# Retention and feed-forward on one core: two retention clusters per group against one, with a GpSimd token between its two output parts

## The chip, the cores and the metric

The kernel runs on one core of a Trainium2 chip. A core has five engines that work side by side, each through its own queue of instructions in order: TensorE (PE in the profile, its weight loads PEld), VectorE (DVE), ScalarE (ACT), GpSimd (POOL) and SyncE (SP), which here issues almost all transfers. They meet only through semaphores: an instruction may wait for counts that other engines or transfers raise. Tiles live in SBUF, on 128 partitions; TensorE writes its results into PSUM, which has eight banks of 512 float32 per partition.

The metric is the device time of one execution in microseconds, the median of several runs. For the kernel before it is 292.66 us (five runs, 292.35 to 292.84). One execution was also taken with the hardware profiler.

## What is computed

A retention layer (attention with a decay in place of a softmax) and, on its output, a feed-forward layer with a squared relu:

```python
# q, k, v: (8, 8, 576, 64)   w_in: (512, 2048)   w_out: (2048, 512)
scores = scale * np.matmul(q, k.transpose(0, 1, 3, 2))
gamma = 1.0 - 2.0 ** (-5.0 - np.arange(H, dtype=np.float32))
Dmat = np.where(rel >= 0, gamma[:, None, None] ** rel[None, :, :], 0.0)
ret = scores * Dmat[None, :, :, :]
attn = np.matmul(ret, v)
x = attn.transpose(0, 2, 1, 3).reshape(B * S, H * D)
r = np.maximum(x @ w_in, 0.0)
out = (r * r) @ w_out
```

Inputs and output are float32; the kernel's matmuls work in fp16.

## The kernel before

**Units and groups.** The 576 positions of a batch are cut into four full units of 128 positions and a rest of 64; the rests of two batches make one tail unit. That gives 36 units, taken two at a time in 18 groups (0 to 17). Units 8, 17, 26 and 35 are tails. Units below 8 (groups 0 to 3) are handled in pairs by other functions, which the change doesn't touch.

**Retention of a unit.** The decay is split into factors of the position, so that a unit needs only a 64x64 masked product inside each half (a chunk) and a running state between chunks. Per unit: GpSimd casts k, q and v to fp16 (`add_unit`; L366 k and q, L378 v with its decay); SyncE transposes k and q by a DMA (L391) into `kqT`. TensorE then makes, in 64x64 pieces through `quad` (L354): *scores* (`psc`, 16 matmuls a unit, bank pair prS), *sums* of k times v for the state (`psS`, 16 for a full unit, none for a tail), and the output `psO` (bank pair prO) in two parts, *out1* and *out2*. out1 and half of out2 multiply q with the states `R` and `Rm`; the other part of out2 multiplies v with the masked scores `rT`. out1 and out2 add into the same places of PSUM from different halves of the array's rows. VectorE masks the scores (`rT`, L658), builds the states (`Rm` L677 and L679, `stmp` L683, `R` L687) and scales the output into `xT` (L719).

`quad` gives TensorE a position in the array: a 64x64 quarter. Everything else on TensorE (feed-forward, transposes of the paired units) uses the whole 128x128 array. A run of 64x64 matmuls between such work is called a cluster here.

**Clusters before.** `add_ret` builds them. For groups 4 to 6 there are two a group: scores and sums of the group, and later out1, a drain of TensorE, and out2. From group 7 (`JOIN = 7`) on the work of neighbouring groups is joined in another way: a first cluster has out1 of group g and scores of g+1, a second, some 2 to 5 us later, has sums of g+1 (into the bank pair prS, after the scores there have been masked) and out2 of g. Group 17 has its outputs alone, with a drain.

**Feed-forward of a group.** `add_ff`: 64 matmuls of 256 columns with w_in (L842, into `ph`, one PSUM bank for eight of them), relu on ScalarE (L850), square on ScalarE for seven of eight banks (L860) or on VectorE (L862), and from group 2 on the second matmul by Strassen's scheme (`add_strassen`): seven products of eight matmuls (L934) on fp16 sums `gS` that VectorE builds (L911), with copies on ScalarE (L947, L1008) and adds on VectorE (L957) into `o`, which SyncE stores. `ph`, the products' `po` and the transposes share the four feed-forward banks (tag "ff").

**What sets the order.** Every piece of work is a task of the class `Schedule`, with an engine, a key (priority), an assumed duration, tasks that it depends on and resources that it takes (`acq`: ff 4, prS 1, prO 1, and counts of buffers). `emit` plays the tasks through with the assumed durations and writes them out in the order in which they started. On the chip each engine works through its list in that order, and semaphores hold it where something is not ready. So a changed key, resource or duration can move instructions on every engine.

Of the kernel before, what the change touches and what calls it, by code (L numbers as in the profile page):

```python
# [15 lines left out]
class Schedule:  # L16
# [4 lines left out]
        self.count = dict(count)  # L21
        self.tasks = []

    def add(self, eng, key, dur, fn, deps=(), acq=(), after=None, lag=0.0):
        t = dict(eng=eng, key=key, dur=dur, fn=fn, acq=acq, n=len(self.tasks), users=[], free=[], lag=lag,
                 left=len(deps), ready=0.0, lat=self.LAT[eng] if after is None else after)
        for d in deps:
            d["users"].append(t)
        self.tasks.append(t)
        return t  # L30
# [11 lines left out]
    def emit(self):  # L42
        ready = {e: [] for e in self.LAT}
        busy = {e: False for e in self.LAT}
        events = []
        order = []
        seq = 0

        def push(at, what, t):
            nonlocal seq  # L50
            seq += 1
            heapq.heappush(events, (at, seq, what, t))
        for t in self.tasks:
            if t["left"] == 0:
                heapq.heappush(ready[t["eng"]], (t["key"], t["n"], t))
        now = 0.0
        while True:
            for e in ready:
                if busy[e]:
                    continue  # L60
                held = []
                while ready[e]:
                    item = heapq.heappop(ready[e])
                    t = item[2]
                    if all(self.count[r] >= t["acq"].count(r) for r in t["acq"]):
                        for r in t["acq"]:
                            self.count[r] -= 1
                        t["start"] = now
                        order.append(t)
                        busy[e] = True  # L70
                        push(now + t["dur"], "end", t)
                        break
                    held.append(item)
                for item in held:
                    heapq.heappush(ready[e], item)
            if not events:
                break
            now = events[0][0]
            while events and events[0][0] <= now + 1e-9:
                _, _, what, t = heapq.heappop(events)  # L80
                if what == "end":
                    busy[t["eng"]] = False
                    for w in t["users"]:

                        push(now + (0.0 if w["eng"] == t["eng"] else t["lat"]), "dep", w)
                    for g in t["free"]:
                        push(now + t["lat"], "free", g)
                elif what == "dep":
                    t["left"] -= 1
                    if t["left"] == 0:  # L90
                        push(now + t["lag"], "go", t)
                elif what == "go":
                    heapq.heappush(ready[t["eng"]], (t["key"], t["n"], t))
                else:
                    t["left"] -= 1
                    if t["left"] == 0:
                        self.count[t["res"]] += 1
        assert len(order) == len(self.tasks)
        for t in order:
            t["fn"]()  # L100
# [3 lines left out]
def kernel(  # L104
# [9 lines left out]
    nc = tc.nc  # L114
# [44 lines left out]
    w_out16 = const.tile([P, NF, DM], FP16, name="w_out16")  # L159


    junk = const.tile([P, 512], FP16, name="junk")
    nc.vector.memset(junk, 0.0)
    ident = const.tile([P, P], FP16, name="ident")
    make_identity(nc, ident)
# [28 lines left out]


    heads = [(4 * n + 2 * a + b, n, a, b) for n in range(2) for a in range(2) for b in range(2)]
    lncol = const.tile([P, NP], FP32, name="lncol")
    lnrow_R = const.tile([P, NP], FP32, name="lnrow_R")
    for h, n, a, b in heads:
        nc.vector.memset(lncol[64 * b:64 * b + 64, 2 * n + a:2 * n + a + 1], lng[h])  # L200
        nc.vector.memset(lnrow_R[64 * a:64 * a + 64, 2 * n + b:2 * n + b + 1], lng[h])

    mask = const.tile([P, 64], FP32, name="mask")
    nc.gpsimd.memset(mask, 1.0)
    for c in range(2):
        nc.gpsimd.affine_select(out=mask[c * 64:(c + 1) * 64], in_=mask[c * 64:(c + 1) * 64],
                                compare_op=ALU.is_ge, fill=0.0, base=0, pattern=[[1, 64]], channel_multiplier=-1)

    mask2 = const.tile([P, 2, 2, 64], FP32, name="mask2")
    nc.gpsimd.memset(mask2, 1.0)  # L210
    for c in range(2):
        for e in range(2):
# [4 lines left out]
    for hp in range(NP):  # L217
# [9 lines left out]
    SQ_ACT = (0, 1, 2, 3, 4, 5, 6)  # L227
    SPREAD = 0.1
    SQ_LATE = (1, 4, 6)
    JOIN = 7  # L230
    LAG = {"v2": 1.2, "w1": 1.3, "k4": 0.7, "q4": 0.5}
    LAG_T, LAG_O = 1.5, 5.0
    PAIRED = 8
    FIRST = ["k0", "q0", "v0", "k2", "q2", "w0", "v2", "w1", "w2", "w3", "w4", "w5", "w6", "w7", "k4", "q4", "v4", "k6", "q6", "v6"]
    sched = Schedule(dict(ff=4, prS=1, prO=1, g=3, ld=5, wst=4, kq=7, v16=7, rT=4, x=3, rl=3, o=4, p1=2, u2=2, u4=2,
                          R=6, Rm=6, kqT=6))
    add = sched.add
    tile_of = {}
    last_load = []
# [110 lines left out]

    def quad(out_, lhsT, rhs, row, col, start=True):
        nc.tensor.matmul(out_, lhsT=lhsT, rhs=rhs, start=start, stop=True, skip_group_check=True,  # L354
                         tile_position=(64 * row, 64 * col))

    def half(x):
        return slice(64 * x, 64 * x + 64)
# [1 line left out]
    def add_unit(u, base):  # L360
# [15 lines left out]
        def fv():  # L376
# [1 line left out]
            nc.gpsimd.tensor_tensor(  # L378
                out=t, in0=tile_of["v32", u],
                in1=vdec[kind].rearrange("p (h o) -> p h o", o=1).to_broadcast([P, H, D]), op=ALU.mult)  # L380
        ck = add("POOL", base, 0.65, fk, deps=[loaded["k", u]], acq=("kq",))
        cq = add("POOL", base + 1, 0.62, fq, deps=[loaded["q", u], ck])
        cv = add("POOL", base + 2, 1.1, fv, deps=[loaded["v", u]] + tail, acq=("v16",))
        for what, t in (("k", ck), ("v", cv)):
            for w in gate.get((what, u), []):
                sched.need(w, t)
# [201 lines left out]
    def emit_sums(g, tag):  # L588

        if not full_of(g):  # L590
            return
        tile_of["psS", g] = ps_ret.tile([P, 2, 512], FP32, name="psS", tag=tag)
        for s, u in enumerate(units_of(g)):
            if u not in full_of(g):
                continue
            ps = tile_of["psS", g][:, :, cols(s)].rearrange("p c (n i) -> p c n i", i=64)
            for hp in range(NP):
                for c, a in ((0, 0), (1, 1), (0, 1), (1, 0)):
                    h = 4 * (hp // 2) + 2 * a + hp % 2
                    quad(ps[half(a), c, hp, :], tile_of["kq", u][half(c), 0, half(2 * hp + a)],  # L600
                         tile_of["v16", u][half(c), h, :], c, a)


# [61 lines left out]
    def after_sums(g, t, key, res):  # L665

        chain = []
        for s, u in enumerate(units_of(g)):
            if u not in full_of(g):
                continue  # L670
            c0 = units[u][2] == 0

            def fr0(s=s, u=u, c0=c0):
                r = tile_of["Rm", u] = st_pool.tile([P, NP * D], FP16, name="Rm", tag="Rm")
                x = tile_of["psS", g][:, 0, cols(s)]
                if c0:
                    nc.vector.tensor_copy(out=r, in_=x)  # L677
                else:
                    nc.vector.tensor_tensor(out=r, in0=x, in1=tile_of["R", u - 1], op=ALU.add)  # L679

            def fr1(s=s, u=u):
                r = tile_of["tmp", u] = work.tile([P, NP * D], FP32, name="stmp", tag="stmp", bufs=1)
                nc.vector.tensor_tensor(out=r, in0=tile_of["psS", g][:, 1, cols(s)], in1=tile_of["Rm", u], op=ALU.add)  # L683

            def fr2(s=s, u=u):
                r = tile_of["R", u] = st_pool.tile([P, NP * D], FP16, name="R", tag="R")
                nc.vector.tensor_tensor(  # L687
                    out=r.rearrange("p (n d) -> p n d", d=D), in0=tile_of["tmp", u].rearrange("p (n d) -> p n d", d=D),
                    in1=dec128.rearrange("p (n o) -> p n o", o=1).to_broadcast([P, NP, D]), op=ALU.mult)
            r0 = add("DVE", key + 0.1 + s, 0.42, fr0, deps=[t] + chain[-1:] + ([] if c0 else [T["R", u - 1]]),  # L690
                     acq=("Rm",))
            if not c0:
                T["Rread", u - 1].append(r0)
            r1 = add("DVE", key + 0.2 + s, 0.42, fr1, deps=[r0])
            r2 = add("DVE", key + 0.3 + s, 0.5, fr2, deps=[r1], acq=("R",))
            chain += [r0, r1, r2]
            T["Rm", u], T["R", u], T["Rread", u], T["Rmread", u] = r0, r2, [], r1
        if chain:
            sched.free(res, [chain[-2]])

    def after_outs(g, t1, t2, key):
# [33 lines left out]
    def add_ret(g):  # L735
# [15 lines left out]
            after_scores(g, t, base + 5)  # L751
            after_sums(g, t, base + 5, "prO")
        if joined(g):
            k = len(groups[g + 1])

            def f1():
                emit_out1(g)
                emit_scores(g + 1)

            def f2():  # L760

                emit_sums(g + 1, "prS")
                emit_out2(g)
            t1 = add("PE", base + 10, 0.2 + QUAD * (8 * n + 16 * k), f1, deps=out1_deps(g) + scores_deps(g + 1),
                     acq=("prO", "prS"))
            after_scores(g + 1, t1, base + 11)
            t2 = add("PE", base + 30, 0.2 + QUAD * (24 * n + 16 * len(full_of(g + 1))), f2,
                     deps=[t1] + T["masked", g] + T["masked", g + 1] + sums_deps(g + 1), acq=("prS",))
            for u in units_of(g + 1):
                T["kqread", u] = t2  # L770
            after_outs(g, t1, t2, base + 30.4)
            after_sums(g + 1, t2, base + 31, "prS")
        else:
            def fb():
                emit_out1(g)
# [7 lines left out]

    HF, HM = NF // 2, DM // 2
    wB = {(i, j): w_out16[:, i * HF:(i + 1) * HF, j * HM:(j + 1) * HM] for i in range(2) for j in range(2)}
    wT = [const.tile([P, HF, HM], FP16, name=f"wT{i}") for i in range(4)]

    def add_wT(i, in0, in1):
        ts = []
# [284 lines left out]
```

## Time and profile before

| What | Value |
|---|---|
| median of five runs | 292.66 us |
| the profiled execution, its own time | 292.8 us |
| its span, first to last instruction | 291.08 us |
| TensorE clock granted | 1.00 |
| wide matmuls with w_in (L842, 128x256) | 1152 |
| wide matmuls of the second layer (L934, 128x256) | 896 |
| relu on ScalarE (L850) | 144 x 589 ns |
| square on ScalarE (L860) | 104 x 631 ns |
| copy of a bank's half on ScalarE (L947, 128x256) | 48, 365 to 370 ns |
| cast of k or q on GpSimd (L366) | 28 + 28, 672 ns mean |
| cast of v on GpSimd (L378, full units) | 24 x 1067 ns |
| xT on VectorE (L719) | 28 x 685 ns |
| mask of scores on VectorE (L658) | 28 x 682 ns |
| transposing DMA (L391), issue to landing | 3.1 / 4.3 / 6.0 us (min, median, max) |

The page lists busy time by engine and by line. For TensorE a matmul's "busy" time is longer than its share of the pace, since matmuls overlap; the distance from one start to the next is the pace. In the timeline each row has the start in us, the length in us, engine, line, operation, output, inputs, shape, count and, in brackets, how long the engine was idle before and what ended that.

### The profile page before, as it was taken

How to read it: one execution, taken by the hardware profiler on the slowest of the kernel's cores; microseconds unless marked ns; L12 is line 12 of the kernel's file. 1: busy time of each engine (PE TensorE's matmuls, PEld its weight loads, DVE VectorE, ACT ScalarE, POOL GpSimd, SP SyncE). 2: the span in 40 equal slices, each digit the busy share in tenths (PEclk: the TensorE clock that was granted, in tenths of full speed). 3: DMA queues.
4: the chain of work that ended last, by engine and by line, in shares of the span. 5: the costliest groups of instructions: out<-in, count | busy, mean ns of one | idle time of the engine just before them, and what ended most of it. 6: DMA issues, size and time to landing. Idle time of an engine off the chain costs nothing.

```text
span 291.1 us, 10071 instructions
## 1 busy us (share of the span) xinstructions
PE 283.5 (97%) x4328; PEld 233.8 (80%) x4328; DVE 197.5 (68%) x430; ACT 187.5 (64%) x356; POOL 89.2 (31%) x125
## 2 busy tenths in 40 slices
PE   7999999999999999999999999999999999999995
PEld 3557765588888888888888888888888888888884
DVE  3877379849495958766768856666786866564632
ACT  6366876385757575867666666756767676747830
POOL 4352455515414333441604241505061500000000
PEclk9999999999999999999999999999999999999999
DMA  7999999999999999998959899959897920201004
GB/s 194 326 351 387 375 283 257 218 189 187 243 159 224 202 178 245 212 219 202 183 141 206 185 215 211 196 146 192 189 184 197 166 77 2 74 2 73 2 0 146
DMA packets 139949, 54.14 MB, mean 186 GB/s; under 512 B 118144, under 2 KB 131968, under 8 KB 139904
## 3 DMA queue, kind: packets, MB, share of 16 engines
q1 hardware_dynamic: 139600, 53.23, 81.1%
q8 instruction: 34, 0.56, 0.8%
q10 hardware_dynamic: 304, 0.26, 0.3%
q14 instruction: 11, 0.09, 0.1%
HBM read 36.70 MB, written 9.44 MB: 159 GB/s over the span
## 4 chain that ended last, share of the span: by engine, by line
PE 89%; DMA 6%; SPq 2%; DVE 1%; issue 1%; POOL 0%; DVEq 0%
PE ph L842 43%; PE po L934 34%; DMA wi<-in_moe_w_in_dram 6%; PE po L882 4%; PE psO L354 4%; SPq L298 2%; PE psc L354 2%; PE psS L354 2%; DVE rx L472 1%; POOL w_in L333 0%; PE psT L429 0%; DVE o L957 0%; DVE p L986 0%; DVE stmp L495 0%; DVE R L500 0%
## 5 line engine op out<-in xcount | busy, mean ns | idle before, releaser
L842 PE MATMUL ph<-xT,w_in 128*128 128x256 f16 x1152 | 139.9, 273 | 0.4 <-POOL w_in L333 0.4
L842 PEld LDWEIGHTS <-w_in 128*128 128x128 f16 x1152 | 110.9, 98 | 15.9 <-POOL w_in L333 0.9
L850 ACT ACTIVATE rl<-ph 128x512 f16<-128x512 f32 x144 | 84.1, 589 | 47.2 <-PE ph L842 45.4
L860 ACT ACTIVATE gT<-rl 128x512 f16<-128x512 f16 x104 | 65.6, 631 | 2.9
L934 PEld LDWEIGHTS <-gS 128*128 128x128 f16 x512 | 49.2, 98 | 6.7 <-DVE gS L911 0.8
L934 PE MATMUL po<-wT,gS 128*128 128x256 f16 x384 | 52.5, 273 | 0.0
L911 DVE TENSOR_TENSOR gS<-gT,gS 128x512 f16<-128x512 f16 x64 | 34.8, 549 | 11.2 <-ACT gT L860 10.6
L934 PEld LDWEIGHTS <-gT 128*128 128x128 f16 x384 | 37.2, 98 | 4.4
L911 DVE TENSOR_TENSOR gS<-gT 128x512 f16<-128x512 f16 x64 | 32.3, 505 | 12.5 <-ACT gT L860 12.4
L934 PE MATMUL po<-w_out,gT 128*128 128x256 f16 x256 | 34.5, 273 | 0.0
L366 POOL CAST kq<-k 128x512 f16<-128x512 f32 x28 | 18.8, 672 | 47.0 <-DMA k<-in_k_dram 40.3
L366 POOL CAST kq<-q 128x512 f16<-128x512 f32 x28 | 18.8, 673 | 44.6 <-DMA q<-in_q_dram 44.5
L862 DVE TENSOR_TENSOR gT<-rl 128x512 f16<-128x512 f16 x40 | 20.6, 519 | 15.7 <-ACT rl L850 15.0
L378 POOL TENSOR_TENSOR v<-v,vdec_full 128x512 f16<-128x512 f32 x24 | 25.6, 1067 | 18.1 <-DMA v<-in_v_dram 16.5
L947 ACT COPY u<-po 128x256 f32<-128x256 f32 x32 | 11.8, 370 | 21.5 <-PE po L934 21.4
L957 DVE TENSOR_TENSOR o<-po,u 128x256 f32<-128x256 f32 x31 | 13.0, 421 | 15.5 <-PE po L934 7.8
L719 DVE TENSOR_TENSOR xT<-psO,gam_full 128x512 f16<-128x512 f32 x28 | 18.9, 685 | 6.0 <-PE psO L354 6.0
L658 DVE TENSOR_TENSOR rT<-psc,mask 128x512 f16<-128x512 f32 x28 | 18.3, 682 | 5.7 <-PE psc L354 5.7
L934 PE MATMUL po<-wT,gT 128*128 128x256 f16 x128 | 17.0, 273 | 0.0
L934 PE MATMUL po<-w_out,gS 128*128 128x256 f16 x128 | 16.9, 273 | 0.0
L882 PE MATMUL po<-w_out,gT 128*128 128x512 f16 x64 | 16.0, 380 | 0.3 <-DVE stmp L495 0.3
L957 DVE TENSOR_TENSOR o<-po,p 128x256 f32<-128x256 f32 x17 | 7.2, 424 | 12.0 <-ACT u L947 5.2
(81 smaller groups left out, 244.5 us busy)
## 6 DMA issues: line engine op xcount, KB each, us to landing
out_dram<-o SPq DMA_DIRECT2D x31, 256.0 KB, 3.4
k<-in_k_dram SPq DMA_DIRECT2D x24, 256.0 KB, 4.4
q<-in_q_dram SPq DMA_DIRECT2D x24, 256.0 KB, 4.8
v<-in_v_dram SPq DMA_DIRECT2D x24, 256.0 KB, 5.0
wo<-in_moe_w_out_dram SPq DMA_DIRECT2D x4, 1024.0 KB, 9.7
wi<-in_moe_w_in_dram SPq DMA_DIRECT2D x3, 1024.0 KB, 8.9
pair<-in_k_dram SPq DMA_DIRECT2D x4, 512.0 KB, 6.9
pair<-in_q_dram SPq DMA_DIRECT2D x4, 512.0 KB, 7.3
```

The source lines that it names most:

```text
L354: nc.tensor.matmul(out_, lhsT=lhsT, rhs=rhs, start=start, stop=True, skip_group_check=True, tile_position=(64 * row, 64 * col))
L366: op(out=out_.rearrange("p (n b a d) -> p n b a d", n=2, b=2, a=2), in_=in_.rearrange("p (n a b) d -> p n b a d", n=2, a=2))
L378: nc.gpsimd.tensor_tensor(out=t, in0=tile_of["v32", u], in1=vdec[kind].rearrange("p (h o) -> p h o", o=1).to_broadcast([P, H, D]), op=ALU. ...
L719: nc.vector.tensor_tensor(out=tile_of["x", g][:, :, s * P:(s + 1) * P].rearrange("p n (c i) -> p c n i", c=2), in0=tile_of["psO", g][:, :, ...
L842: nc.tensor.matmul(tile_of["ph", g, fb][:, j, :], lhsT=w_in16[:, m, fi * P:(fi + 1) * P], rhs=tile_of["x", g][:, m, :], start=(m == 0), st ...
L850: nc.scalar.activation(out=t, in_=tile_of["ph", g, fb], func=ACTF.Relu)
L860: nc.scalar.activation(out=t, in_=rl, func=ACTF.Square)
L862: nc.vector.tensor_tensor(out=t, in0=rl, in1=rl, op=ALU.mult)
L882: nc.tensor.matmul(tile_of["po", u], lhsT=tile_of["g", g][:, fi, s * P:(s + 1) * P], rhs=w_out16[:, fi, :], start=(fi == 0), stop=(fi == N ...
L911: nc.vector.tensor_tensor(out=Sx(k, h), in0=in0(h), in1=in1(h), op=op)
L934: nc.tensor.matmul(tile_of["pb", g, bank], lhsT=left(i), rhs=right[:, i, :], start=(start and i == 0), stop=(i == HF - 1), skip_group_chec ...
L957: nc.vector.tensor_tensor(out=o_tile(u)[:, half * HM:(half + 1) * HM], in0=bank(x), in1=tile_of[name, g], op=ALU.add)
```

## The change

- `JOIN` is 5: groups 5 to 16 are joined.
- A joined group has one cluster instead of two: out1 of g, scores of g+1, sums of g+1, out2 of g, in this order.
- Between out1 and out2 a GpSimd instruction (`pass_turn`: a memset of one element, `token`) waits for out1's last matmul, and out2's first matmul waits for it.
- The sums go into two feed-forward banks (one per row half) in place of prS. If both units of g+1 are full, ScalarE copies the second unit's half of both banks into an SBUF tile `sums`, from which VectorE builds that unit's state.
- The planner gets a resource "pool" (1), which the casts of units from 8 on and the joined cluster take in turn, and a flag `firm`: a firm task that waits for resources keeps others from taking them.
- Keys change: the cluster's (`CLUSTER = 26`), those of masks, `xT` and the second part of the states (`K_MASK`, `K_X`, `K_ST`).
- `junk`, the operand of the warm-up matmuls, is now part of `wT[0]`, and the masks are fp16.

In the order that results, TensorE has the same stream up to group 4's output, and the same matmuls after that. On GpSimd there are 12 memsets, each behind the casts that its cluster reads (five of them behind one or two casts of the next unit too); on SyncE some transposes, stores and loads change places.

```diff
-    def add(self, eng, key, dur, fn, deps=(), acq=(), after=None, lag=0.0):
+    def add(self, eng, key, dur, fn, deps=(), acq=(), after=None, lag=0.0, firm=False):
...
+        kept = {}
+        LASTING = ("pool",)
...
+                kept = {r: t for r, t in kept.items() if r in LASTING}
...
-                    if all(self.count[r] >= t["acq"].count(r) for r in t["acq"]):
+                    if all(kept.get(r, t) is t for r in t["acq"]) and all(self.count[r] >= t["acq"].count(r) for r in t["acq"]):
...
+                            kept.pop(r, None)
...
+                    if t["firm"]:
+                        kept.update((r, t) for r in t["acq"] if r not in kept)
...
-    junk = const.tile([P, 512], FP16, name="junk")
+    wT = [const.tile([P, NF // 2, DM // 2], FP16, name=f"wT{i}") for i in range(4)]
+    junk = wT[0][:, 0:2].rearrange("p f m -> p (f m)")
...
-    mask = const.tile([P, 64], FP32, name="mask")
+    mask = const.tile([P, 64], FP16, name="mask")
...
-    JOIN = 7
+    JOIN = 5
+    CLUSTER = 26
+    K_MASK, K_X, K_ST = 30, 8, 30
...
+    def pass_turn():
+        last = issued[-1]
+        mark = nc.gpsimd.memset(token, 0.0)
+        after(mark, last)
+        return mark
...
-        ck = add("POOL", base, 0.65, fk, deps=[loaded["k", u]], acq=("kq",))
-        cq = add("POOL", base + 1, 0.62, fq, deps=[loaded["q", u], ck])
-        cv = add("POOL", base + 2, 1.1, fv, deps=[loaded["v", u]] + tail, acq=("v16",))
+        ck = add("POOL", base, 0.65, fk, deps=[loaded["k", u]], acq=("kq", "pool"))
+        cq = add("POOL", base + 1, 0.62, fq, deps=[loaded["q", u], ck], acq=("pool",))
+        cv = add("POOL", base + 2, 1.1, fv, deps=[loaded["v", u]] + tail, acq=("v16", "pool"))
+        for x in (ck, cq, cv):
+            sched.free("pool", [x])
...
-        tile_of["psS", g] = ps_ret.tile([P, 2, 512], FP32, name="psS", tag=tag)
+        if tag == "ff":
+            tile_of["psS", g] = [ps_ff.tile([P, 512], FP32, name="psS", tag="ff") for c in range(2)]
...
+        aside = res == "ff" and len(us) == 2
+        copies = {}
+        if aside:
+            def fc(c):
+                def f():
+                    if c == 1:
+                        tile_of["sums", g] = work.tile([P, 2, 256], FP32, name="sums", tag="sums", bufs=1)
+                    nc.scalar.copy(out=tile_of["sums", g][:, c], in_=tile_of["psS", g][c][:, cols(1)])
+                return f
+            copies[1] = add("ACT", key, 0.37, fc(1), deps=[t], acq=("sums",))
+            copies[0] = add("ACT", key + 0.01, 0.37, fc(0), deps=[copies[1]])
...
+        if aside:
+            sched.need(copies[0], chain[0])
+            sched.free("ff", [copies[0]])
+            sched.free("ff", [chain[1]])
+            sched.free("sums", [chain[-2]])
...
         if joined(g):
-            k = len(groups[g + 1])
-
-            def f1():
+            n1 = len(full_of(g + 1))
+
+            def f():
                 emit_out1(g)
+                mark = pass_turn()
                 emit_scores(g + 1)
-
-            def f2():
-
-                emit_sums(g + 1, "prS")
+                emit_sums(g + 1, "ff")
+                turn.append(mark)
                 emit_out2(g)
-            t1 = add("PE", base + 10, 0.2 + QUAD * (8 * n + 16 * k), f1, deps=out1_deps(g) + scores_deps(g + 1),
-                     acq=("prO", "prS"))
-            after_scores(g + 1, t1, base + 11)
-            t2 = add("PE", base + 30, 0.2 + QUAD * (24 * n + 16 * len(full_of(g + 1))), f2,
-                     deps=[t1] + T["masked", g] + T["masked", g + 1] + sums_deps(g + 1), acq=("prS",))
+            t = add("PE", base + CLUSTER, 0.17 + QUAD * (32 * n + 16 * len(groups[g + 1]) + 16 * n1), f,
+                    deps=out1_deps(g) + T["masked", g] + scores_deps(g + 1) + sums_deps(g + 1),
+                    acq=("prO", "prS", "pool") + (("ff", "ff") if n1 else ()), firm=True)
+            sched.free("pool", [t])
+            after_scores(g + 1, t, base + CLUSTER + K_MASK)
             for u in units_of(g + 1):
-                T["kqread", u] = t2
-            after_outs(g, t1, t2, base + 30.4)
-            after_sums(g + 1, t2, base + 31, "prS")
+                T["kqread", u] = t
+            after_sums(g + 1, t, base + CLUSTER + 0.5, "ff")
+            after_outs(g, t, t, base + CLUSTER + K_X)
```

## The prediction, made before the changed kernel ran

> **What bounds the kernel now.** I read the page first (busy shares, slices, the chain that ended last), then the timeline of TensorE around the lines that the diff touches, then the rows that price a signal between engines.
>
> ```profile
> PE 283.5 (97%) x4328; PEld 233.8 (80%) x4328; DVE 197.5 (68%) x430; ACT 187.5 (64%) x356; POOL 89.2 (31%) x125
> ...
> PE   7999999999999999999999999999999999999995
> ...
> PEclk9999999999999999999999999999999999999999
> ...
> PE 89%; DMA 6%; SPq 2%; DVE 1%; issue 1%; POOL 0%; DVEq 0%
> ```
>
> From about 25 us to the end TensorE never rests, at full clock, and the chain is 89% TensorE. So an edit counts for what it does to TensorE's own stream, or if it makes TensorE wait. The timeline shows where the stream has holes:
>
> ```profile
> 152.14 1.04 PE L934 MATMUL po<-w_out,gT 128*128 128x256 f16 x8
> 153.02 1.04 PE L934 MATMUL po<-wT,gS 128*128 128x256 f16 x8
> 153.89 1.47 PE L842 MATMUL ph<-xT,w_in 128*128 128x256 f16 x12
> ...
> 158.69 1.04 PE L934 MATMUL po<-wT,gS 128*128 128x256 f16 x8
> 159.66 0.21 PE L354 MATMUL psO<-kqT,Rm 64*64 64x64 f16 x1
> ...
> 160.17 0.61 PE L842 MATMUL ph<-xT,w_in 128*128 128x256 f16 x4
> 160.62 1.04 PE L934 MATMUL po<-w_out,gS 128*128 128x256 f16 x8
> 161.49 1.04 PE L934 MATMUL po<-wT,gT 128*128 128x256 f16 x8
> 162.46 0.45 PE L354 MATMUL psS<-v,kq 64*64 64x64 f16 x32
> ...
> 163.23 3.67 PE L842 MATMUL ph<-xT,w_in 128*128 128x256 f16 x32
> ```
>
> The first column is the start, so starts give the pace. Sixteen wide matmuls take 1.75 us (152.14 to 153.89): 0.109 each, 0.875 for eight. Where 64x64 work follows, eight take 0.97 (158.69 to 159.66; 161.49 to 162.46): entering a retention cluster costs 0.095. Inside, the 48 small matmuls of the group's first cluster take 0.51 and the 80 of its second 0.77 (to 163.23). The difference gives 0.0081 for a small matmul, and 0.51 - 48 x 0.0081 = 0.12 is fixed. A cluster thus costs 0.21 us beside its matmuls. I find no other hole of weight: outside clusters the wide matmuls keep 0.109, with three slips of 0.1 to 0.2 us after 64 us.
>
> **The change, part by part.**
>
> 1. *Fewer clusters.* Before, groups 7 to 16 have two each. After, one with the same small matmuls (16 out1, 32 scores, 32 sums, 48 out2; fewer with tail units): 10 x 0.21 = 2.1 us saved.
>
> 2. *Groups 5 and 6 join.* Before, outputs 5, scores and sums 6, outputs 6, scores and sums 7 are four clusters. After, two: 2 x 0.21 = 0.42. Also gone are the two drains between the output parts:
>
> ```profile
> 87.10 0.19 PE L354 MATMUL psO<-kqT,Rm 64*64 64x64 f16 x1
> ...
> 87.39 0.32 PE L354 MATMUL psO<-rT,v 64*64 64x64 f16 x16
> ...
> 87.99 0.61 POOL L366 CAST kq<-k 128x512 f16<-128x512 f32 x1 [1.15 <-PE psO L354]
> 88.11 1.29 DVE L719 TENSOR_TENSOR xT<-psO,gam_full 128x512 f16<-128x512 f32 x2 [0.32 <-PE psO L354]
> ```
>
> Group 5's cluster takes 0.93 for 64 matmuls (86.97 to 87.90), where 64 without a drain take 0.65 (94.55 to 95.20): 0.28. Group 6's takes 0.90 for 56 (102.05 to 102.95) against 0.12 + 56 x 0.0081 = 0.57: 0.33. Together 0.61. Parts 1 and 2: 2.1 + 0.42 + 0.61 = 3.13 us off.
>
> 3. *The token.* In each of the 12 joined clusters GpSimd waits for out1's last matmul, writes one element, and the first weight load of out2 waits for that. Four steps, from rows: a small matmul takes 0.19 (87.10). TensorE's end to GpSimd's start: the last small matmul ends at 87.97, the cast starts at 87.99: 0.02. From the second token on the instruction carries two waits; VectorE's xT, with two, starts 0.14 after 87.97, so I add 0.1. The write itself and GpSimd to TensorE:
>
> ```profile
> 0.31 0.10 POOL L1058 MEMSET const-float32-0.0<- 128x1 f32 x1 [0.31 <-issue]
> ...
> 18.38 1.57 POOL L410 TENSOR_TENSOR vx<-pair,vdec_pair 128x512 f16<-128x512 f32 x1 [2.13 <-DMA pair<-in_v_dram]
> ...
> 20.00 0.29 PE L354 MATMUL psS<-vx,kx 64*64 64x64 f16 x12 [0.61 <-POOL vx L410]
> ```
>
> 0.10, and 0.05 (19.95 to 20.00). Sum 0.19 + 0.02 + 0.10 + 0.10 + 0.05 = 0.46 from the start of out1's last matmul. The cover is scores and sums: 65 steps x 0.0081 = 0.53 in nine clusters, 49 x 0.0081 = 0.40 in the three whose next group has a tail unit (7, 12, 16). An exposed weight load adds something (its row is 0.11, of which 0.02 to 0.05 shows, by the spacing of the first rows of a cluster). I take 0.03 x 9 + 0.10 x 3 = 0.57. Bounds: 0 (all covered) and 0.1 x 9 + 0.18 x 3 = 1.44 (the whole weight load exposed).
>
> What stands ahead of the token in GpSimd's queue are the casts of the group that the cluster needs anyway, and in some clusters from group 10 on one or two casts of the next unit. Behind it wait the next six casts, 2 x (0.67 + 0.67 + 1.07) = 4.8 us of GpSimd, and behind them on SyncE two transposes (4.3 us to landing, up to 6.0) and the stores and loads queued after them. Next late would be the next cluster's scores. For units 16 and 17: cluster 6 at about 104.4 (TensorE's order at the pace above), token over by 105, fifth cast 3.8 later, transpose landed by 115, cluster 7 at about 117.3. So 2 us remain where this is tightest, and I take 0. If that cover were gone, TensorE would wait the excess in each cluster.
>
> 4. *A GpSimd write against VectorE.* [...]
>
> ```profile
> 77.65 1.04 POOL L378 TENSOR_TENSOR v<-v,vdec_full 128x512 f16<-128x512 f32 x1 [0.42 <-DMA v<-in_v_dram]
> 78.13 0.85 DVE L911 TENSOR_TENSOR gS<-gT,gS 128x512 f16<-128x512 f16 x1 [1.87 <-ACT gT L860]
> 78.64 0.81 POOL L366 CAST kq<-k 128x512 f16<-128x512 f32 x1
> ```
>
> The add takes 0.85 instead of 0.42, the cast 0.81 instead of 0.61. A token behind one add would be up to 0.42 late. But in VectorE's new order only PSUM-reading adds (o<-po) stand between the last such add and the cluster, group 5 apart. Bounds 0 and 12 x 0.42 = 5.0; nearest is the PSUM-reading add (0.41 beside casts, nobody stretched), so 0 here, kept as a rival. [...]
>
> 5. *Sums in feed-forward banks.* They hold two of four. ScalarE copies out the second unit's half: 2 x 0.37 a cluster, nine full clusters, 6.7 us on an engine 64% busy; hidden, since its long waits are for ph (45.4 us). If that cover were gone, 0.74 a cluster. VectorE runs add (0.42), x (0.69), add (0.42), x (0.69): both banks are back some 1.7 us after the cluster, x is done at 2.3. TensorE fills a ph bank per 0.875, so it wants the third at 1.75; x is wanted earliest in group 5, after 12 ph and 16 po matmuls, 3.06. Banks are the close call: bounds 0 and 0.25 x 12 = 3.0 (one slip like the largest seen); by the three slips now, 0.2 in all. VectorE's two adds from the SBUF copy may stretch from 0.42 to 0.85 beside casts: 0.86 a cluster at 68% busy, hidden; uncovered, they would make the Strassen sums late.
>
> 6. *Small edits.* A weight load with two waits takes 0.05 on TensorE's queue; five clusters now have one in mid-stream, 0 to 0.25, I take 0.13. The fp16 masks (0.68 now; nearest all-fp16 add 0.42), junk inside wT touch no wait of TensorE. Scores come some 3 us later in a group, and masks (after x) and states behind them; all are read only in the next cluster, some 14 us on: 0; uncovered, each us late would be a us of that cluster's wait.
>
> Sum: -3.13 + 0.57 + 0.2 + 0.13 = -2.23 us. The profiled span 291.08 becomes 288.85. That execution took 292.8, the median of the runs is 292.66; what lies around the span stays, so 292.66 - 2.23 = **290.4**. Extremes without the rivals: 292.66 - 3.13 = 289.5, and with 1.44, 0.25 and 0.6 of bank slips, 291.8.
>
> **The rivals.**
>
> *A: the fixed 0.12 is paid per part, not per cluster.* Each cluster now has two parts, the new one four. Against it: the 64-matmul cluster (0.65) and the 80-matmul one fit one line. For it: none has four parts. Then only 0.095 a cluster goes: 12 x 0.095 + 0.61 = 1.75; with costs of 0.9, 292.66 - 0.85 = 291.8.
>
> *B: the banks eat it.* Two banks out of four gone for 1.7 us while ScalarE (7 of 8 squares) works off relu. A slip of 0.25 in every cluster gives back 3.0, so 292.66 - 2.23 - 0.2 + 3.0 = 293.2 at worst; with half, 291.7. It decides from 0.19 a cluster (2.23 / 12): no change, 292.6. For it: x, sums and copies crowd just there. Against: no ph wait of weight in 144 banks now.
>
> *C, the slower side: the token is late.* If a cast or an fp16 add holds GpSimd when out1 ends, TensorE stands in mid-cluster. At 0.42 in each of twelve: 292.66 - 2.23 + 5.0 = 295.4. It turns slower once the token is 0.19 later than I count. For it: GpSimd works in order, and its casts wait for DMA 107 us in sum. Against: its casts for a cluster now end 8 to 14 us before the scores.
>
> **How the numbers follow.** Forecast 0.65 (own range 289.5 to 291.4), A 0.12, B 0.11, C 0.12. A measurement of this kernel tells 0.2% (0.59 us) from no change. Faster takes the forecast, three quarters of A and a little of B: 0.76; the rest of A and most of B: 0.12 same; C: 0.12 slower. The range runs from 289.4, all hidden, to 292.4, which takes in A and half of B and leaves C out.
>
> **What would show it.** Right: one cluster per group from the sixth, 128 small matmuls in about 1.2 us with a step below 0.1 before out2; 12 clusters fewer; no drain within groups 5 and 6; wide matmuls still at 0.109 after a cluster; span near 288.9. Wrong: a hole of 0.2 or more before out2 with GpSimd as releaser (C); ph weight loads that wait for ScalarE or VectorE after a cluster (B); more than 1.4 us without one hole (A); scores that wait for kqT.

## The result, and the profile after

The changed kernel takes 293.0 us (median of 28 runs, 292.45 to 294.24), the kernel before 292.62 beside it (48 runs). The ratio is 1.0017, with a 95% interval of 1.001 to 1.0024: no gain, and if anything a loss of 0.17%. The forecast was 290.4 with a range of 289.4 to 292.4. It was wrong.

From the page of the changed kernel: busy time, two rows of slices, the queue that brings instructions, the chain that ended last, and the token's group.

```profile
PE 282.7 (97%) x4328; PEld 235.5 (81%) x4328; DVE 189.9 (65%) x430; ACT 193.0 (66%) x374; POOL 87.2 (30%) x137
...
PE   8999999999999999999999999999999999999994
...
PEclk9999999999999999999999999999999999999999
...
q8 instruction: 34, 0.56, 0.9%
...
PE 81%; DMA 12%; DVE 2%; SPq 2%; issue 1%; POOL 0%; DVEq 0%
...
L380 POOL MEMSET token<- 1x1 f32 x12 | 1.1, 88 | 108.9 <-PE psO L367 108.9
```

The page looks as before: TensorE at 97%, full clock, nothing on VectorE, ScalarE or GpSimd that has filled up. The span is 291.5 us against 291.08. The row to look at twice is the fourth, which is much the same before the change: 34 packets with 0.56 MB, 16 KB each. TensorE has 8,656 weight loads and matmuls, and 8,656 / 34 is 255. Kernel 3 below, with 508 more, has 36 packets. The same row before:

```profile
q8 instruction: 34, 0.56, 0.8%
```

What has changed is seen in the list of TensorE's waits after 60 us (line, tile, releaser; sum, number of waits, longest). For the kernel before this list is empty. After:

```profile
PE psO L367 <- issue: 0.7, 1, 0.7
PE ph L898 <- issue: 0.6, 1, 0.6
PE po L990 <- issue: 0.2, 1, 0.2
```

Three waits, and none of them for an engine, a transfer or a bank: "issue" means that the profile finds nothing that TensorE waited for. The timeline of TensorE around the first of them, cluster 8 (start, duration, operation):

```profile
131.39 1.04 PE L898 MATMUL ph<-xT,w_in 128*128 128x256 f16 x8
...
132.51 0.43 PE L367 MATMUL psc<-kqT 64*64 64x64 f16 x32
132.81 0.45 PE L367 MATMUL psS<-v,kq 64*64 64x64 f16 x32
132.82 0.09 POOL L380 MEMSET token<- 1x1 f32 x1 [9.63 <-PE psO L367]
...
133.07 0.32 PE L367 MATMUL psO<-rT,v 64*64 64x64 f16 x16
...
133.26 0.35 PE L367 MATMUL psO<-rT,v 64*64 64x64 f16 x14
...
134.34 0.22 PE L367 MATMUL psO<-rT,v 64*64 64x64 f16 x2 [0.72 <-issue]
...
134.35 0.28 PE L367 MATMUL psO<-kqT,R 64*64 64x64 f16 x8
...
134.55 0.88 PEld L898 LDWEIGHTS <-w_in 128*128 128x128 f16 x9
```

The token is written at 132.82 to 132.91, while the sums still run, and out2 begins at 133.07 right behind the last of them: that part works. Then, in the middle of out2, between the 14th and 15th of sixteen equal matmuls, TensorE stands. From start to start the three steps are 0.92, 0.86 and 0.50 where 0.03 to 0.11 is usual, together 2.0 us lost. The 15th matmul waits for no semaphore and uses the tile that the 14th used. The second hole lies in plain ph matmuls behind cluster 9, as empty of causes:

```profile
148.77 1.04 PE L898 MATMUL ph<-xT,w_in 128*128 128x256 f16 x8
150.40 0.81 PE L898 MATMUL ph<-xT,w_in 128*128 128x256 f16 x6 [0.59 <-issue]
```

Eight matmuls take 0.87 by their pace, so the ninth is due at 149.64 and starts at 150.40.

What these places have in common is seen when TensorE's program is counted through, each weight load and each matmul as one instruction, a second wait as another. The trace also has the start of every packet of the instruction queue:

| step begins | TensorE resumes with instruction | that number mod 256 | last instruction packet starts | from there to the resumption |
|---|---|---|---|---|
| 133.43 | 4027 | 187 | 131.56 | 2.79 us |
| 149.53 | 4539 | 187 | 147.61 | 2.79 us |
| 181.80 | 5564 | 188 | 179.55 | 2.75 us |

By these counts the program arrives in blocks of 256 instructions (16 KB), each stall lies on a block's border, and here TensorE goes on 2.75 to 2.79 us after a fetch began. The count of the table leaves out TensorE's drains. With them, and taking the first instruction that is late, be it a weight load or a matmul, the three are 4034, 4546 and 5570, each 194 mod 256. After 60 us a fetch begins about when TensorE crosses the border before the one where its block is needed, between 1.4 us ahead of it and 2.8 us behind. In wide matmuls 256 instructions last 14 us (128 times 0.109), five times those 2.8. A joined cluster of 128 small matmuls is 256 instructions and lasts 1.27 us, less than half of them. So, as a theory (the block theory): if a border falls close to the cluster's end, the next block is used up before the one behind it has come. The experiments test it. The kernel before had clusters of 88 to 160 instructions with 2 us or more of wide work between; its tightest border between 60 and 280 us had 0.4 us to spare.

### The profile page after: what moved, and what is told of

The parts are those of the page before. It is cut to its first block, busy times and chain, and to the rows that moved or that the text cites. A ratio compares the mean times of both kernels' runs of the same rounds, so it can differ in the third digit from the quotient of the medians.

```text
span 291.5 us, 10097 instructions
## 1 busy us (share of the span) xinstructions
PE 282.7 (97%) x4328; PEld 235.5 (81%) x4328; DVE 189.9 (65%) x430; ACT 193.0 (66%) x374; POOL 87.2 (30%) x137
## 4 chain that ended last, share of the span: by engine, by line
PE 81%; DMA 12%; DVE 2%; SPq 2%; issue 1%; POOL 0%; DVEq 0%
PE ph L898 39%; PE po L990 33%; DMA wi<-in_moe_w_in_dram 6%; PE psO L367 4%; DMA pair<-in_v_dram 3%; DMA wo<-in_moe_w_out_dram 3%; SPq L308 2%; PE psc L367 2%; PE psS L367 1%; PE po L938 1%; DVE wT L849 1%; DVE rx L501 1%; POOL w_in L343 0%; DVE o L1013 0%; DVE vx L439 0%
## 5 line engine op out<-in xcount | busy, mean ns | idle before, releaser
L990 PEld LDWEIGHTS <-gS 128*128 128x128 f16 x512 | 49.8, 98 | 6.1 <-DVE gS L967 0.2
L967 DVE TENSOR_TENSOR gS<-gT 128x512 f16<-128x512 f16 x64 | 31.4, 493 | 16.8 <-ACT gT L916 16.8
L967 DVE TENSOR_TENSOR gS<-gT,gS 128x512 f16<-128x512 f16 x64 | 30.5, 476 | 7.9 <-ACT gT L916 7.1
L380 POOL MEMSET token<- 1x1 f32 x12 | 1.1, 88 | 108.9 <-PE psO L367 108.9
L405 POOL TENSOR_TENSOR v<-v,vdec_full 128x512 f16<-128x512 f32 x24 | 26.3, 1096 | 10.3 <-DMA v<-in_v_dram 10.2
L918 DVE TENSOR_TENSOR gT<-rl 128x512 f16<-128x512 f16 x40 | 18.1, 456 | 14.7 <-ACT rl L906 14.3
L393 POOL CAST kq<-q 128x512 f16<-128x512 f32 x28 | 17.8, 634 | 6.1 <-DMA q<-in_q_dram 5.9
L691 DVE TENSOR_TENSOR rT<-psc,mask 128x512 f16<-128x512 f32 x28 | 18.9, 679 | 0.3 <-PE psc L367 0.3
```

Source lines behind the costliest of these rows:

```text
L393: op(out=out_.rearrange("p (n b a d) -> p n b a d", n=2, b=2, a=2), in_=in_.rearrange("p (n a b) d -> p n b a d", n=2, a=2))
L405: nc.gpsimd.tensor_tensor(out=t, in0=tile_of["v32", u], in1=vdec[kind].rearrange("p (h o) -> p h o", o=1).to_broadcast([P, H, D]), op=ALU. ...
L691: nc.vector.tensor_tensor(out=r, in0=tile_of["psc", g][:, :, cols(s)].rearrange("p a (n i) -> p a n i", i=64), in1=mask.rearrange("p (o r ...
L918: nc.vector.tensor_tensor(out=t, in0=rl, in1=rl, op=ALU.mult)
L967: nc.vector.tensor_tensor(out=Sx(k, h), in0=in0(h), in1=in1(h), op=op)
L990: nc.tensor.matmul(tile_of["pb", g, bank], lhsT=left(i), rhs=right[:, i, :], start=(start and i == 0), stop=(i == HF - 1), skip_group_chec ...
```

## The experiments

All nine kernels compute the full result. A median stands beside the one of the kernel before in the same group of runs. Kernels 1, 2, 6 and 8 ran together (before: 292.45), then 3, 4 and 7 (292.62), then 5 and 9 (292.76).

**1. Move the borders off the clusters.** The same multiplications, some of them issued in two halves:

```diff
-  for m in range(NP):
-      nc.tensor.matmul(ph[:, j, :], lhsT=w_in16[...], rhs=x[:, m, :], start=(m == 0), stop=(m == NP - 1))
+  for m in range(NP):
+      parts = 2 if n == 2 and g >= JOIN and m and 3 * fi + m - 1 < 14 else 1
+      for c in range(parts):      # w = n * P // parts columns each
+          nc.tensor.matmul(ph[:, j, c*w:(c+1)*w], lhsT=w_in16[...], rhs=x[:, m, c*w:(c+1)*w],
+                           start=(m == 0), stop=(m == NP - 1 and c == parts - 1))
```

> Same work; from group 5 on 14 of each group's ph matmuls are issued as two of 128 columns with the same weights, 28 instructions more in a group, so that a full group has 524 and the blocks of 256 instructions in which TensorE's program arrives keep their borders off the ends of the clusters. Block theory (TensorE stood at 133.4, 149.5 and 181.8 us because a merged cluster uses up a block faster than the next one arrives): worked out from the order of the instructions, no block then holds a whole cluster, the three steps of 0.92, 0.86 and 0.50 are gone and nothing like them comes elsewhere; 293.0 - 2.0 = 291.0, between 290.7 and 291.4. Rival, data or PSUM banks that come late at these places: nothing that the clusters wait for is changed, so the steps stay in clusters 8, 9 and 11 and the time is 293.0. Rival, splitting is not free: up to 0.055 for each of 182 extra matmuls, 293 to 303.

Measured: 291.24 us (290.93 to 291.38), 0.995 of before (interval 0.9937 to 0.9963), span 289.4. Cluster 8 in this kernel:

```profile
133.11 0.32 PE L367 MATMUL psO<-rT,v 64*64 64x64 f16 x16
...
133.31 0.37 PE L367 MATMUL psO<-rT,v 64*64 64x64 f16 x16
133.49 0.25 PE L367 MATMUL psO<-kqT,R 64*64 64x64 f16 x8
133.68 3.23 PE L901 MATMUL ph<-xT,w_in 128*128 128x256 f16 x28
```

The sixteen matmuls are whole again, and TensorE's list of waits after 60 us is empty. From 85 us on the tightest border has 1.1 us to spare. Adding 364 instructions made the kernel 1.8 us faster than the change as made, and faster than the kernel before.

**2. Move the borders somewhere else.** Nothing is done but to start the stream differently:

```diff
-  nc.tensor.matmul(warm_ps[0], lhsT=junk[:, 0:P], rhs=junk, ...)
+  for c in range(4 if late else 1):     # the last 24 of 40 warm-up matmuls, 128 columns each
+      nc.tensor.matmul(warm_ps[0][:, c*w:(c+1)*w], lhsT=junk[:, 0:P], rhs=junk[:, c*w:(c+1)*w], ...)
```

> Same work; 24 of the warm-up matmuls on junk before the kernel's own work are issued as four of 128 columns, so 144 more instructions stand ahead of everything and every block border moves 144 instructions earlier in the work. Block theory: the steps at 133, 150 and 182 us vanish, and new ones without a releaser come where the borders now fall near a cluster's end: at about 91 to 95, 106 to 110, 205 to 209 and 220 to 224 us, in clusters 5, 6, 13 and 14; in sum 2.7 to 5.9 instead of 2.0, so 293.5 to 296. Rival, late data or banks, or transfers that collide in DMA: the steps stay where they are, and the time is 293.0.

Measured: 295.22 us (294.26 to 295.58), 1.0089 of before (1.0074 to 1.0104). The steps at 133, 150 and 182 are gone. The profiled execution (the fastest of the six) has new ones in clusters 13 and 14: 1.84 at 206.55 and 0.27 at 223.62, at instructions 6588 and 7100, both 188 mod 256, resuming 2.78 and 2.64 us after a fetch began. The first:

```profile
205.82 0.24 PE L373 MATMUL psO<-kqT,Rm 64*64 64x64 f16 x4
205.99 0.83 PE L904 MATMUL ph<-xT,w_in 128*128 128x256 f16 x6
208.39 0.83 PE L904 MATMUL ph<-xT,w_in 128*128 128x256 f16 x6 [1.57 <-issue]
```

Clusters 5 and 6, foreseen too, got by; the borders there had 1.1 and 0.2 us to spare. Two early steps had not been foreseen: 0.74 at 16.34 us and 1.78 at 21.77 us, where the extra warm-up and an early cluster share a block. By 65 us this kernel is 1.5 us behind kernel 1. So the time lies in the foreseen range partly by luck: the steps after 60 us give 1.9 us, less than the 2.7 to 5.9 foreseen, and the early ones made up for it. By the count with drains all four are 194 mod 256, and so are the stalls after 60 us in kernels 3, 6 and 8. The stalls move with the count of instructions; late data, banks or transfers would have left them in clusters 8, 9 and 11.

**3. The worst place.** Kernel 1 with the warm-up of kernel 2.

> The same kernel as e1_align with nothing changed but its place in the instruction stream: 24 warm-up matmuls on junk are issued as four each, 144 instructions more ahead of everything. Since a group is about two blocks long here, the borders now meet nearly all 12 clusters at the same bad place instead of none. Block theory, worked out from the order of the instructions, the 2.77 us from a fetch to its use and a request that is 0.3 to 1.1 us late: steps without a releaser in 8 to 12 clusters, 0.3 to 2.4 us each, in sum 6 to 21; with the sizes seen in e2_moved about 12, so 303, between 297 and 312. Rival, the splits themselves make e1_align fast (shorter matmuls, better feed): 291.2, as there.

Measured: 299.28 us (297.52 to 299.89), 1.0202 of before (1.0171 to 1.0232): 8 us more than kernel 1 for the same work in the same order. After 60 us the profile has six new steps, at 136.64, 152.34, 182.57, 199.38, 214.19 and 228.66, all at 187 or 188 mod 256, resuming 2.6 to 2.9 us after a fetch began, 5.5 us in sum. That is less than the 6 to 21 expected; the time is at the low end of its range, and only with what follows. The other 3.0 us fell before 65 us: the early stalls of kernel 2, worth 1.5 there, and behind them this (stretch; length, busy times, granted clock, DMA share, GB/s):

```profile
24.00:28.30 4.30, 4.21 (x41) 3.02 (x38) 3.19 (x5) 2.13 (x3) 1.94 (x2) 0.60 1.05 385
```

The granted clock averaged 0.60 over these 4.3 us. In kernel 2, after the same gap, it stayed at 1.00.

**4. Are the halves a gain by themselves?** The kernel before with the split of kernel 1.

> The kernel before with the same 14 splits in each group from group 5 on, and no other change. Its clusters are 96 to 160 instructions long with 2 us or more of wide work between, so by the block theory it had no stall to lose: 292.5, within 0.3 of the kernel before. Rival, the splits bring a gain of their own: about 291.0.

Measured: 292.96 us against 292.62, ratio 1.0009 (0.9999 to 1.0019). That is 0.34 by the medians, where 0.3 was the most expected. The halves bring nothing where there is no stall to lose, and cost a little. (The profiled execution, the slowest of the twelve, also waits 0.3 once for VectorE's masks, at 149 us.) Kernel 1's ph matmuls, two whole and six in halves:

```profile
123.98 1.05 PE L901 MATMUL ph<-xT,w_in 128*128 128x256 f16 x14
124.87 0.60 PE L995 MATMUL po<-wT,gS 128*128 128x256 f16 x4
```

They take 0.89 where eight whole ones take 0.87: some 0.003 a split, 0.4 to 0.5 us for 182.

**5. Another length.** Kernel 1 with 16 splits per group.

> e1_align with 16 matmuls split in each group instead of 14, so that a full group is 528 instructions long. By the block theory both keep all borders off the cluster ends, so no step without a releaser from 85 us on, and 291.2 again (290.9 to 291.5). If e1_align was a lucky draw of something else that depends on its length: anything from 291 to 296.

Measured: 291.51 us against 292.76, ratio 0.9957 (0.9944 to 0.9971), no step without a releaser after 85 us. Kernel 1 was no lucky draw.

**6. A drain in the token's place.**

```diff
-                mark = pass_turn()
...
-                turn.append(mark)
+                nc.tensor.drain()
                 emit_out2(g)
```

> GpSimd's token is left out; in its place TensorE drains ahead of out2 in each of the 12 joined clusters, as in groups 5 and 6 before. If the token is hidden behind scores and sums (what the trace of the changed kernel shows), a drain costs its whole 0.28, 12 times 3.3, less some 0.6 in the two clusters where TensorE stands for its instructions behind it: 295.5 to 296.4. If the token costs 0.05 a cluster as forecast: 295.1 to 295.8. If it costs 0.28 or more a cluster (rival C): 293.0 or faster.

Measured: 294.57 us (294.12 to 295.52), 1.007 of before (1.005 to 1.009). In cluster 9 the drain looks like this:

```profile
147.67 0.44 PE L367 MATMUL psS<-v,kq 64*64 64x64 f16 x32
148.28 0.34 PE L367 MATMUL psO<-rT,v 64*64 64x64 f16 x17 [0.16 <-issue]
```

The sums' 32 matmuls and the drain take 0.61 from start to start, against 0.28 for the sums alone in the changed kernel. All 12 clusters together are 3.35 us longer than those of kernel 1, 0.28 each: the whole price of a drain, so the token costs almost nothing. The time rose by 1.6 only. Two of the changed kernel's three stalls were gone with the slower clusters, and so were two slips of 0.1 and 0.2 behind VectorE's sums at 81 and 93 us. The third, on the same border, grew from 0.86 to 1.31; the profile names VectorE's xT for it, but that was done 0.29 before TensorE went on. The time is below every range of the expectation, which had the drain right and what would be regained behind it too small. The profiled execution, the slowest of the four, is 2.2 longer than that of the changed kernel.

**7. A later token.**

```diff
         after(mark, last)
+        for _ in range(2):
+            mark = nc.gpsimd.memset(token, 0.0)
         return mark
```

> e1_align with three writes of the token in a row instead of one; each waits for the one before, so the token comes some 0.28 us later (two writes of 0.088 and two waits of about 0.05). By the trace the token is over 0.13 to 0.22 us before out2's first matmul in nine clusters, where a token that is waited for takes 0.055 (the three clusters with a tail unit next), so the slack is 0.08 to 0.16 in the nine and nothing in the three. Token theory: 3 times 0.28 plus 9 times 0.12 to 0.20, 1.9 to 2.6: 293.1 to 293.8. If the slack is larger than the trace shows or nobody waits for the token: 291.2.

Measured: 293.07 us against 292.62, ratio 1.0012 (1.0002 to 1.0021); 1.8 us above kernel 1, just below the range. Cluster 10:

```profile
161.99 0.45 PE L367 MATMUL psS<-v,kq 64*64 64x64 f16 x32
162.00 0.09 POOL L380 MEMSET token<- 1x1 f32 x1 [9.11 <-PE psO L367]
162.14 0.23 POOL L383 MEMSET token<- 1x1 f32 x2
...
162.43 0.32 PE L367 MATMUL psO<-rT,v 64*64 64x64 f16 x16
```

The sums used to take 0.26; out2 now starts 0.44 after them, 0.06 after the last write ended (162.14 + 0.23). Over 12 clusters TensorE waits 2.7 us more ahead of out2, but the clusters are only 1.9 longer: after such a wait the small matmuls run faster (late in a cluster 0.0079 each against 0.0083), as told at the end.

**8. Leave groups 5 and 6 apart.** JOIN = 7 instead of 5, the rest as changed.

> Groups 5 and 6 keep separate clusters with a drain, as in the kernel before; from group 7 on all is as in the changed kernel. The forecast's second step gave joining them 0.42 for two entries and 0.61 for two drains; with 0.1 of more cost inside each joined cluster and the slip of 0.14 in group 6, 0.6 to 0.8 is left: 293.6 to 293.8. If joined clusters gain nothing: 293.0. The number of instructions ahead of each later cluster stays nearly the same, so by the block theory the steps stay in clusters 8, 9 and 11.

Measured: 293.87 us (292.2 to 294.39), 1.0037 of before (1.0024 to 1.0049). By the ratios joining the two is worth 0.2%, 0.6 us (the two intervals leave 0.2 to 1.0), as expected. That holds as far as the stalls cost the same in both: here 1.04 at 134.35 and 0.96 at 165.50, some 1.9 us lost against 2.0. They sit in clusters 8 and 10, not in 8, 9 and 11 as expected: the count of instructions alone did not tell which borders are missed. In the changed kernel, too, a fetch begins anywhere between 1.4 us ahead of a border and 2.8 behind it.

**9. Sums ahead of scores.** The two middle parts of kernel 1 exchanged.

> e1_align with the two middle parts of a joined cluster exchanged: out1, sums, scores, out2; the same instructions, and TensorE's program keeps its length. A joined cluster of 128 takes 1.27 us where 48 in 0.51 and 80 in 0.78 lead to 1.18. Theory: 0.05 of the 0.09 is the first weight load of the sums, which has two waits; then the step of 0.06 moves from the 48th small matmul to the 17th in those clusters, and the rest, the slower pace late in a cluster, stays; time 291.2 (290.9 to 291.5), since the pause only moves. Rival, the step belongs to a place about 48 matmuls in, where TensorE has used up the instructions that were issued ahead: it stays at the 48th, in whatever part.

Measured: 291.39 us against 292.76, ratio 0.9952 (0.9939 to 0.9964), the time of kernel 1. Both readings fall: the step of 0.06 is neither at the 17th nor at the 48th matmul but gone, and a cluster of 128 takes 1.25 instead of 1.27. In kernel 1, too, the one cluster of 128 without the two waits takes 1.25. So the two waits of that weight load cost 0.02 net, and the other 0.07 of the 0.09 too much is in the pace.

## Why the prediction was wrong, step by step

**What was not in it.** The sum took the supply of the stream itself for granted: a small matmul costs 0.0081 wherever it stands. Steps 1 and 2 pack up to 128 of them together, and TensorE's program no longer arrives as fast as it is used (256 instructions in 1.27 us, against some 2.8 from a fetch to its use). That costs 2.0 us in the profiled execution (span 291.5, and 289.4 in kernel 1, where only the borders are moved). It was none of the rivals, and no row of the trace of before showed such a stall; the row of the instruction queue, with the count of instructions in a cluster, was the only trace of it. No extreme of the sum reached above 291.8, for the same reason. This term, taken as nothing without a reason, is the step that failed. The mis-sized clusters below cost the forecast another 0.8, which alone would have left the time inside the range.

**Steps 1 and 2, clusters: mis-sized.** Foreseen 3.13 us, less 0.57 for the token: 2.56. From the start of the last wide matmul ahead to the first behind, less one ordinary step, the 24 clusters of before against the 12 of kernel 1 give 1.186 for groups 7 to 16 and 0.558 for 5 and 6, together 1.74. Two clusters of 48 and 80 (0.51 + 0.78, and 0.093 of entry each) become one of 128 (1.27 + 0.093), which saves 0.11 where the forecast had 0.21 less 0.03 to 0.10 for the token. The entry and the two drains went as told; of the fixed 0.12 nearly all is paid again inside. Rival A's sum of 1.75 is the measured saving, but by luck: A had the cost at every new part, and in cluster 8 of kernel 1 the step into scores is 0.022 and into out2 0.004, no more than between other small matmuls. The cost is in the slower pace and in the weight load with two waits (kernel 9). A's time of 291.8 had costs of 0.9 in it that did not come.

**Step 3, the token: over-priced.** The chain was right: 0.48 from the start of out1's last matmul to out2 (0.19 for the matmul, 0.14 to the write, 0.088 for it, 0.055 back) against 0.46. But the cover is longer, since the cluster runs slower than 0.0081. In nine clusters nothing is exposed; in the three with a tail unit next out2 starts 0.03, 0.06 and 0.06 late. In all 0.15 instead of 0.57. Kernels 6 and 7 agree: a drain costs its full price, and a token that is 0.29 later is felt in every cluster.

**Step 4, GpSimd held by VectorE: right.** All twelve writes take 0.088 and start at most 0.15 after out1's end. Rival C fell. In the trace of the changed kernel VectorE ran a PSUM-reading add (o<-po,u) beside seven of the twelve writes and an fp16 add beside none, so what such an add does to a lone write was not measured.

**Step 5, banks: right in kind.** No ph matmul waits for ScalarE or VectorE after a cluster. Rival B fell. The two slips at 81 and 93 us are waits of po for VectorE's Strassen sums, of the size that before had too.

**Step 6, small edits: 0.13 foreseen.** Five clusters have the weight load with two waits; at 0.02 net (kernel 9) it is 0.1.

**The sum as it came.** By the profiled spans: 1.7 us gained by clusters and token, 2.0 lost at the borders of instruction blocks, small slips for the rest: 291.08 became 291.5. With the borders moved the gain stays: 289.4. By the medians kernel 1 is 1.2 us faster than before, not 1.7. The profiled execution of before was a long one (span 291.08; the median span of the 17 runs beside kernel 1 is 290.7), that of kernel 1 an ordinary one. A saving of 1.74 less 0.4 to 0.5 for the splits agrees with 1.2. Two slips of 0.15 within out2 of groups 6 and 14, not on a border, stay open.

## What to carry to other kernels

Where many short instructions stand close together, count them: here a block was 256 instructions, and at the stalls TensorE went on 2.5 to 3.0 us after its packet's start. A stretch that used up a block faster (1.27 us) depended on where the borders fell, and an edit far ahead shifted them (144 instructions more in the warm-up, kernel 2). A stall with no releaser, at the same instruction count modulo 256, is the sign here, and splitting a few long instructions, which cost 0.4 to 0.5 us in all here, is a way to shift it. And a fixed cost read as a difference of two short stretches need not be saved by one long stretch.

## What the runs showed of the hardware

- **Instruction blocks.** TensorE's program came in 16 KB packets of 256 instructions, and it resumed 2.5 to 3.0 us after the packet's start in all stalls on a border listed above; one border of kernel 2, at 240.28 us, was crossed 2.4 us after it without a step. The same work took from 291.2 to 299.3 us by the place of the borders; about 1.5 of these 8.1 us came with the slower clock told below.
- **Splitting is nearly free.** A wide matmul issued as two of 128 columns with the same weights, each half with its own weight load, adds some 0.003 us to 0.109 (kernel 1: 0.89 against 0.87 us with six splits).
- **Two paces of small matmuls.** Early in a cluster of the changed kernel TensorE runs four 64x64 matmuls in 0.032 us (0.0079 each); later, from the 60th to 90th on, it falls to 0.0083, with single steps of 0.035 and 0.025 around the 110th. After the longer token wait of kernel 7 it runs at 0.0079 nearly to the end of the cluster. With kernel 1's slips in groups 6 and 14 mostly gone, this refunds 0.8 of 2.7 us. What sets the slower pace was not tried.
- **The clock after a gap.** After an equal 1.56 us gap at 22 us the granted clock averaged 0.60 over 4.3 us in one kernel (3) and 1.00 in another (2). Why is open.
